# PSUM banks of the expert stage sorted by role, with banks of their own for h of each expert's first tile

## The chip, the cores and the metric

The kernel runs on one core of a Trainium2 chip. The core has five instruction queues that run side by side and meet through semaphores: TensorE (PE, matrix products and transposes), VectorE (DVE), ScalarE (ACT), GpSimd (POOL) and SyncE (SP, which starts most DMA transfers). PE writes its results to PSUM, which has eight banks of 2 KB on each of 128 partitions. The metric is device time in microseconds (us) of one execution. Stated is the median of several runs.

## What is computed

Attention over 16 heads with a block-causal mask, a dense feed-forward layer, and then a mixture of eight experts with one expert per token. The change is in the last part:

```python
def _moe2_ref(x, w_gate, w1, w2, capacity):       # x: 1152 x 512, 8 experts, capacity 288
    logits = x @ w_gate
    expert_idx = np.argmax(logits, axis=1)
    probs = softmax(logits)                        # written out in the original
    gate_w = probs[np.arange(N), expert_idx]
    # token i takes the next free slot of its expert, if one is left: disp[e, slot] = x[i]
    h = np.maximum(np.einsum('ecd,edf->ecf', disp, w1), 0.0)    # w1: 8 x 512 x 1024
    y = np.einsum('ecf,efd->ecd', h, w2)                        # w2: 8 x 1024 x 512
    out[i] = gate_w[i] * y[expert_idx[i], pos[i]]               # 0 for tokens without a slot
```

## The kernel before

The kernel has three parts: attention (`part1`), the feed-forward layer with the router (`part2`), and the experts (`part3`). Parts one and two take the first 340 us. In `part3` every engine executes its instructions in the order in which the code is written; a tile framework adds the semaphore waits that the data and the reuse of buffers need. A pool with `bufs=2` hands out two buffers in turn, and the first instruction that writes a buffer waits until the readers of its last content are done.

Each float32 product is made of three passes: a number is split into a high and a low part (`xh`, `xl` for weights, `dh`, `dl` for tokens, `gh`, `gl` for the hidden layer), and high*high, high*low and low*high are added. ACT makes the high parts, DVE the low ones (line 87 is the helper for that).

The loop of `part3` runs over the experts e. The slots of an expert lie in three tiles j of 128, 128 and 32 slots; `compute(e, j)` is called an *arm* here. Arm 0 runs if the expert has any token, arm 1 if it has more than 128 and arm 2 if it has more than 256. The conditions are branches that each engine takes for itself from a count loaded into its registers (line 1251). An arm that is not taken has a stand-in on each engine that waits until that engine's work so far is done and then adds to the engine's semaphore counter what the arm would have counted. In the profile, waits for it and for the branch appear as `ACTq L1288`, `PEq L1288` and the like: the queue of that engine, not an instruction of it.

An arm does on PE, in this order: 12 matmuls for the first half of the hidden layer (`hx`, line 1193), 6 for the second half, four transposes `hT` of the first half (line 1204), 6 more `hx`, 6 matmuls of the second layer (`acc`, line 1214), `hT` of the second half, 6 `acc`, in arm 0 the transposes `dT` of the next expert's tile 0 (line 1163), and 12 `acc`. Between them ACT applies the relu (`hr`, line 1199, from the `hx` bank), makes `gh` from `hT` (line 1208) and scales the result (`o`, line 1240, from `acc`); DVE makes `gl` from `hT` and `gh`. `o` then goes to the output by an indirect DMA from POOL. In arm 0 six of eight pieces of the next expert's weights are converted as well: `side` gives ACT's halves (`xh`, line 1116) and DVE's (`xl`) to `run` at fixed places of the arm, three of each at its beginning, ahead of the first `hr` on ACT and the first `gl` on DVE. The last two pieces are converted behind arm 0.

Between arm 0 of one expert and arm 0 of the next stand, on every engine: arm 1 or its stand-in, `turn_slots(e + 1, 1)` (four `dT`, then `dh` on ACT and `dl` on DVE), arm 2 or its stand-in, `turn_slots(e + 1, 2)`, and the load of the next count.

The PSUM pools of `part3` have two banks each: `ps_acc` for `acc`, `ps_l1` for `hx`, `ps_m` for `hT` and for `dT` of tile 0, `ps_t` for `dT` of tiles 1 and 2.

Of the kernel before, what the change touches and what calls it, by code (L numbers as in the profile page):

```python
# [9 lines left out]
FP32 = mybir.dt.float32  # L10
# [7 lines left out]
PSUM = bass.MemoryType.PSUM  # L18
# [24 lines left out]
def attention_ffn_moe(  # L43
# [19 lines left out]
    KD = DM // 128  # L63
# [22 lines left out]
    def split_lo(eng, lo, x, hi):  # L86
        eng.tensor_tensor(out=lo, in0=x, in1=hi.bitcast(FP32), op=ALU.subtract)  # L87
# [1032 lines left out]
    def part3():  # L1120
        y_stack.close()
        p3 = ExitStack()
# [1 line left out]
        raw_q = p3.enter_context(tc.tile_pool(name="raw_q", bufs=8, side="right"))  # L1124
        dp = p3.enter_context(tc.tile_pool(name="dp", bufs=2, side="right"))
        hp = p3.enter_context(tc.tile_pool(name="hp", bufs=2, side="right"))
        ps_acc = p3.enter_context(tc.tile_pool(name="ps_acc3", bufs=2, space=PSUM))
        ps_l1 = p3.enter_context(tc.tile_pool(name="ps_l13", bufs=2, space=PSUM))
        ps_m = p3.enter_context(tc.tile_pool(name="ps_m3", bufs=2, space=PSUM))
        ps_t = p3.enter_context(tc.tile_pool(name="ps_t3", bufs=2, space=PSUM))  # L1130
        stiles = [(128 * i, min(128, CP - 128 * i)) for i in range(CT)]
        dT = state["dT"]
# [25 lines left out]
        def turn_slots(e, j):  # L1158

            r, (hi, lo), gt, (s0, n) = rows[e], dT[j], gate[e], stiles[j]  # L1160
            ps = (ps_t if j else ps_m).tile([128, KD, 128], FP32, tag="m", name="dT")
            for kk in range(KD):
                nc.tensor.transpose(  # L1163
                    out=ps[:, kk, 0:n], in_=r[0:n, j, kk * 128:(kk + 1) * 128], identity=ident[0:n, 0:n]
                )
            nc.scalar.activation(out=hi, in_=ps[:, :, 0:n], func=ACTF.Copy)
            split_lo(nc.vector, lo, ps[:, :, 0:n], hi)
            nc.gpsimd.tensor_copy(out=gt[0:n, j, 0:1], in_=r[0:n, j, DM:DM + 1])  # L1168
            nc.gpsimd.tensor_copy(out=gt[0:n, j, 1:2].bitcast(I32), in_=r[0:n, j, DM + 1:DM + 2].bitcast(I32))  # L1169

        def passes(x, w):
            return [(x[0], w[0]), (x[0], w[1]), (x[1], w[0])]

        def compute(e, j, side=(), turn_next=lambda: None):


            s0, n = stiles[j]
            h, hr, g = {}, {}, {}
            his, los = ([x[y] for x in side] for y in range(2))
            acc = ps_acc.tile([128, DM], FP32, tag="acc", name="acc")  # L1180

            def run(fs, k):
                for f in fs[:k]:
                    f()
                del fs[:k]

            def l1(c, half):

                if half == 0:
                    h[c] = ps_l1.tile([128, 512], FP32, tag="l1", name="hx")  # L1190
                todo = [(x, y, kk) for x, y in ((0, 0), (0, 1), (1, 0)) for kk in range(KD)]
                for i, (x, y, kk) in list(enumerate(todo))[6 * half:6 * half + 6]:
                    nc.tensor.matmul(  # L1193
                        out=h[c][0:n], lhsT=dT[j][x][:, kk], rhs=xw[e, 2 * kk][y][:, 0, c * 512:(c + 1) * 512],
                        start=(i == 0), stop=(i == len(todo) - 1),
                    )
                if half == 1:
                    hr[c] = hp.tile([128, 512], FP32, tag="hr", name="hr", bufs=3)
                    nc.scalar.activation(out=hr[c][0:n], in_=h[c][0:n], func=ACTF.Relu)

            def turn(c):
                ps = ps_m.tile([128, 4, 128], FP32, tag="m", name="hT")
                for i in range(4):
                    nc.tensor.transpose(  # L1204
                        out=ps[:, i, 0:n], in_=hr[c][0:n, i * 128:(i + 1) * 128], identity=ident[0:n, 0:n]
                    )
                g[c] = gh, gl = [hp.tile([128, 4, 128], F32R, tag="g" + x, name="g" + x) for x in "hl"]
                nc.scalar.activation(out=gh[:, :, 0:n], in_=ps[:, :, 0:n], func=ACTF.Copy)  # L1208
                split_lo(nc.vector, gl[:, :, 0:n], ps[:, :, 0:n], gh[:, :, 0:n])

            def l2(c, half):
                for f in range(4 * c + 2 * half, 4 * c + 2 * half + 2):
                    for i, (x, y) in enumerate(passes(g[c], xw[e, f // 2 * 2 + 1])):
                        nc.tensor.matmul(  # L1214
                            out=acc[0:n], lhsT=x[:, f % 4, 0:n], rhs=y[:, f % 2, :],
                            start=(f == 0 and i == 0), stop=(f == NF - 1 and i == 2),
                        )

            run(his, 3)
            run(los, 3)  # L1220
            l1(0, 0)
            l1(0, 1)
            run(his, 1)
            l1(1, 0)
            turn(0)
            run(his, 1)
            run(los, 2)
            l1(1, 1)
            l2(0, 0)
            run(his, 1)  # L1230
            turn(1)
            run(los, 1)
            l2(0, 1)
            run(his, NX)
            turn_next()
            run(los, NX)
            l2(1, 0)
            l2(1, 1)
            y = hp.tile([128, DM], FP32, tag="hr", name="o", bufs=3)
            nc.scalar.mul(y[0:n], acc[0:n], gate[e][0:n, j, 0:1])  # L1240
            nc.gpsimd.indirect_dma_start(  # L1241
                out=views[e * CT + j],
                out_offset=bass.IndirectOffsetOnAxis(ap=gate[e][0:n, j, 1:2].bitcast(I32), axis=0),
                in_=y[0:n],
                in_offset=None,
                bounds_check=NT - 1,
                oob_is_err=False,
            )
# [10 lines left out]
        for e in range(E):  # L1259
# [10 lines left out]
            def turn_next():  # L1270
                if new:
                    turn_slots(e + 1, 0)
# [14 lines left out]
            for j in range(1, CT):  # L1287
                with tc.If(count[e] > 128 * j):  # L1288
                    compute(e, j)
                if new:  # L1290
                    turn_slots(e + 1, j)
# [12 lines left out]
    with tc.manual_schedule(engines=every):  # L1304
        part3()
# [27 lines left out]
```

## Time and profile before

| | before |
|---|---|
| median of 3 runs | 520.35 us (519.45 to 522.28) |
| the profiled execution | 521.78 us |
| its span, first to last instruction | 520.1 us |
| PE busy | 493.7 us (95%) |
| DVE busy | 341.7 us (66%) |
| ACT busy | 312.0 us (60%) |
| POOL busy | 117.2 us (23%) |

The profiler recorded one execution. The difference between its time and its span lies before the first and behind the last instruction. A timeline row gives the start, the time, the engine, the line, the operation, the tile written, the tiles read and the number of instructions merged into the row; what stands in brackets is the time that the engine sat idle just before, and what ended it. PE's matmuls overlap, so the time of a single one is longer than the distance from one to the next. The granted clock is the share of full speed that the chip gave TensorE in a stretch; it has two levels, 1.2 and 2.4 GHz, and shares between one half and one are mixtures.

Twelve arms run with this input: arm 0 of experts 0 to 6, arm 1 of experts 0, 4, 5 and 6, and arm 2 of expert 5. Expert 7 has no token.

### The profile page before, as it was taken

To read this page: it belongs to the slowest core of one execution; us is meant where nothing else is said; L and a number is where in the kernel's file an instruction comes from. 1 tells how busy PE (TensorE), PEld (TensorE's weight loads), DVE (VectorE), ACT (ScalarE), POOL (GpSimd) and SP (SyncE) were. 2 spreads that over 40 slices of the span, in tenths; PEclk is the share of its full clock that TensorE was granted. 3 is DMA by queue.
4 is the path that set the end of the run, shared out by engine and by line. 5 is a ranking of instruction groups with operands and counts; after the bars stand their busy time and mean duration, and the time that the engine had idled before them with its cause. 6 is when DMAs were issued, how large, how long until landed. Compare 5 with 4: busy or idle time off the path is not lost. (4 is left out here: it accounts for less than half of the span.)

```text
span 520.1 us, 8710 instructions
## 1 busy us (share of the span) xinstructions
PE 493.7 (95%) x2842; PEld 409.2 (79%) x2842; DVE 341.7 (66%) x828; ACT 312.0 (60%) x699; POOL 117.2 (23%) x219
## 2 busy tenths in 40 slices
PE   7999999999999999999999999889989989999994
PEld 6678877879998889888898888767767768786683
DVE  4479898969987999974554366563565866461351
ACT  4569898867866656753553455374656765562551
POOL 6266777651000000000000112500131230100211
PEclk9589999999999999999999999889979889999999
DMA  8757766503789884430140043377488767180110
GB/s 195 171 125 189 188 146 151 151 4 122 186 256 227 266 284 139 121 122 0 42 122 2 14 129 142 103 255 301 152 299 314 273 245 276 55 337 20 30 43 23
DMA packets 61254, 80.86 MB, mean 155 GB/s; under 512 B 33170, under 2 KB 33170, under 8 KB 61200
## 3 DMA queue, kind: packets, MB, share of 16 engines
q1 hardware_dynamic: 58368, 75.18, 47.9%
q0 software_dynamic: 1632, 4.72, 2.4%
q8 instruction: 28, 0.46, 0.4%
q10 hardware_dynamic: 1200, 0.30, 0.3%
q14 instruction: 26, 0.21, 0.1%
HBM read 62.17 MB, written 12.41 MB: 143 GB/s over the span
## 5 line engine op out<-in xcount | busy, mean ns | idle before, releaser
L260 PE MATMUL acc<-wbh,gh 128*128 128x512 f32 x144 | 57.3, 398 | 0.0
L260 PE MATMUL acc<-wbh,gl 128*128 128x512 f32 x144 | 57.1, 397 | 0.0
L260 PE MATMUL acc<-wbl,gh 128*128 128x512 f32 x144 | 57.1, 397 | 0.0
L904 POOL DMA_INDIRECT disp<-y_all,slot x9 | 9.1, 1013 | 201.1 <-DVE e L245 178.3
L87 DVE TENSOR_TENSOR xl<-rb,xh 128x1024 fp32r<-128x1024 f32 (+1 forms) x36 | 38.9, 1100 | 22.2 <-ACT xh L1116 22.2
L476 POOL TENSOR_SCALAR prob<-prob,stat 128x576 f32<-128x576 f32 (+3 forms) x80 | 41.9, 536 | 35.7 <-DVE stat L470 21.5
L449 ACT ACTIVATE prob<-s,stat 128x288 f32<-128x288 f32 (+4 forms) x96 | 45.3, 479 | 1.7 <-DVE stat L464 1.1
L243 ACT ACTIVATE e<-h 128x384 f32<-128x384 f32 x48 | 23.2, 483 | 36.4 <-PE h L233 34.0
L186 DVE SCALAR_TENSOR_TENSOR cv_t<-r,cv_t 128x512 int32<-128x512 int32 x64 | 44.1, 689 | 0.3
L87 DVE TENSOR_TENSOR xl<-ra,xh 128x1024 fp32r<-128x1024 f32 (+1 forms) x36 | 39.3, 1101 | 7.1 <-ACT xh L1116 6.2
L233 PE MATMUL h<-xh,wah 128*128 128x384 f32 x192 | 42.3, 341 | 0.9 <-DVE e L245 0.9
L436 DVE TENSOR_REDUCE stat<-s 128x1 f32<-128x288 f32 (+4 forms) x96 | 37.7, 422 | 8.2 <-PE s L425 5.7
L233 PE MATMUL h<-xl,wah 128*128 128x384 f32 x192 | 41.6, 337 | 0.0
L233 PE MATMUL h<-xh,wal 128*128 128x384 f32 x192 | 41.1, 336 | 0.0
L245 DVE SCALAR_TENSOR_TENSOR e<-e,h 128x384 f32<-128x384 f32 x48 | 26.3, 549 | 21.2 <-ACT e L244 21.0
L1214 PE MATMUL acc<-xh,gh 128*128 128x512 f32 (+1 forms) x96 | 39.3, 410 | 0.0
L1193 PE MATMUL hx<-xh,dh 128*128 128x512 f32 (+1 forms) x96 | 30.3, 442 | 9.4 <-ACTq L1288 7.2
L233 PEld LDWEIGHTS h<-xh,wah 128*128 128x128 f32 x192 | 34.1, 188 | 6.2 <-DVE e L245 2.4
L1241 POOL DMA_INDIRECT out<-o,gt x12 | 11.7, 972 | 117.7 <-ACT o L1240 40.5
L1214 PE MATMUL acc<-xh,gl 128*128 128x512 f32 (+1 forms) x96 | 38.0, 395 | 0.0
L1214 PE MATMUL acc<-xl,gh 128*128 128x512 f32 (+1 forms) x96 | 37.8, 394 | 0.0
L87 DVE TENSOR_TENSOR gl<-hT,gh 128x512 fp32r<-128x512 f32 (+1 forms) x24 | 15.8, 658 | 33.4 <-ACT gh L1208 33.4
(171 smaller groups left out, 1204.5 us busy)
## 6 DMA issues: line engine op xcount, KB each, us to landing
ra<-in_moe_w SPq DMA_DIRECT2D x32, 512.0 KB, 5.5
rb<-in_moe_w SPq DMA_DIRECT2D x32, 512.0 KB, 6.4
r<-in_moe_w_in SPq DMA_DIRECT2D x16, 512.0 KB, 5.4
r<-in_moe_w_out SPq DMA_DIRECT2D x16, 512.0 KB, 4.0
disp<-z SPq DMA_DIRECT2D x18, 257.0 KB, 6.8
rows<-disp SPq DMA_DIRECT2D x14, 257.0 KB, 3.2
out<-z SPq DMA_DIRECT2D x9, 256.0 KB, 4.3
kr<-in_k SPq DMA_DIRECT2D x16, 128.0 KB, 2.6
```

The source lines that it names most:

```text
L87: eng.tensor_tensor(out=lo, in0=x, in1=hi.bitcast(FP32), op=ALU.subtract)
L186: nc.vector.scalar_tensor_tensor(out=st["t"], in0=x(), scalar=scalar, in1=st["t"], op0=op, op1=ALU.bitwise_or)
L233: nc.tensor.matmul(out=h[:, f, :], lhsT=w[:, kk, (f0 + f) * 128:(f0 + f + 1) * 128], rhs=x[:, kk, t0:t0 + n], start=(i == 0), stop=(i == l ...
L243: nc.scalar.activation(out=e, in_=hf, func=ACTF.Relu, scale=-1.0)
L245: nc.vector.scalar_tensor_tensor(out=e, in0=e, scalar=-1.0, in1=hf, op0=ALU.add, op1=ALU.max)
L260: nc.tensor.matmul(out=acc[t], lhsT=x[:, f, t * 128:(t + 1) * 128], rhs=w[:, f0 + f, :], start=(first and f == 0 and i == 0), stop=(last a ...
L436: nc.vector.tensor_reduce(out=stat[n][0][0:nq, t + b:t + b + 1], in_=banks[n, part, b][0:nq, c0:c0 + w], axis=AX.X, op=ALU.max, negate=True,)
L449: nc.scalar.activation(out=prob[n, part][0:nq, c0 + k0:c0 + k0 + w], in_=banks[n, part, b][0:nq, c0:c0 + w], func=ACTF.Exp, bias=stat[n][0 ...
L476: nc.gpsimd.tensor_scalar(out=p, in0=p, scalar1=stat[n][2][0:nq, t:t + 1], scalar2=0.0, op0=ALU.mult, op1=ALU.add)
L1193: nc.tensor.matmul(out=h[c][0:n], lhsT=dT[j][x][:, kk], rhs=xw[e, 2 * kk][y][:, 0, c * 512:(c + 1) * 512], start=(i == 0), stop=(i == len( ...
L1214: nc.tensor.matmul(out=acc[0:n], lhsT=x[:, f % 4, 0:n], rhs=y[:, f % 2, :], start=(f == 0 and i == 0), stop=(f == NF - 1 and i == 2),)
L1241: nc.gpsimd.indirect_dma_start(out=views[e * CT + j], out_offset=bass.IndirectOffsetOnAxis(ap=gate[e][0:n, j, 1:2].bitcast(I32), axis=0), ...
```

## The change

PSUM has eight banks before and after. `ps_acc` and `ps_m` go from two banks to one each. `ps_l1` becomes a list of two pools of two banks: the first for `hx` of arm 0, the second for `hx` of arms 1 and 2. `dT` of tile 0 moves from `ps_m` to `ps_t`, which then serves `dT` of all three tiles with two banks.

```diff
-        ps_acc = p3.enter_context(tc.tile_pool(name="ps_acc3", bufs=2, space=PSUM))
-        ps_l1 = p3.enter_context(tc.tile_pool(name="ps_l13", bufs=2, space=PSUM))
-        ps_m = p3.enter_context(tc.tile_pool(name="ps_m3", bufs=2, space=PSUM))
+        ps_acc = p3.enter_context(tc.tile_pool(name="ps_acc3", bufs=1, space=PSUM))
+        ps_l1 = [p3.enter_context(tc.tile_pool(name=f"ps_l1{i}3", bufs=2, space=PSUM)) for i in range(2)]
+        ps_m = p3.enter_context(tc.tile_pool(name="ps_m3", bufs=1, space=PSUM))
         ps_t = p3.enter_context(tc.tile_pool(name="ps_t3", bufs=2, space=PSUM))
...
-            ps = (ps_t if j else ps_m).tile([128, KD, 128], FP32, tag="m", name="dT")
+            ps = ps_t.tile([128, KD, 128], FP32, tag="m", name="dT")
...
-                    h[c] = ps_l1.tile([128, 512], FP32, tag="l1", name="hx")
+                    h[c] = ps_l1[j > 0].tile([128, 512], FP32, tag="l1", name="hx")
```

No instruction is added, removed or moved on any engine; what changes is which semaphores instructions wait for, and up to what count. On PE, at the passage from expert 0 to expert 1, there stands before the change (`dh_2031` and `dl_2032` are the two halves of tile 0's tokens; names ending in `_49` are the engines' and DMA queues' semaphores):

```order
L1163 MATMUL dT<-ident,rows 128x32 [waits DMAHW6_49]
L1163 MATMUL dT<-ident,rows 128x32 x3
L1251 TENSOR_LOAD count
L1251 ISA x2
L1274 COMPARE_AND_BRANCH
L1193 MATMUL hx<-xh,dh_2031 128x512 [waits Activation_49]
L1193 MATMUL hx<-xh,dh_2031 128x512 x3
L1193 MATMUL hx<-xl,dh_2031 128x512 [waits DVE_49] x4
L1193 MATMUL hx<-xh,dl_2032 128x512 [waits DVE_49]
```

And at the same place after the change, where the lines are two higher:

```order
L1165 MATMUL dT<-ident,rows 128x32 [waits DMAHW6_49,DVE_49,PE_49]
L1165 MATMUL dT<-ident,rows 128x32 x3
L1253 TENSOR_LOAD count
L1253 ISA x2
L1276 COMPARE_AND_BRANCH
L1195 MATMUL hx<-xh,dh_2031 128x512 [waits Activation_49]
L1195 MATMUL hx<-xh,dh_2031 128x512 x3
L1195 MATMUL hx<-xl,dh_2031 128x512 x4
L1195 MATMUL hx<-xh,dl_2032 128x512 x4
```

The last `dT` waits for DVE as well, and the waits of `hx` for DVE, which that one covers, are gone. The first `hx` waits for ACT's semaphore both times, but up to another count: 477 before, which is reached inside arm 2 (or by its stand-in), and 468 after, which is reached with `o` of arm 0.

## Rows read from the trace of the kernel before

**Rows 1.** Who waited for whom from 340 to 520 us, PE: us in all, times, longest

```profile
PE hx L1193 <- ACTq L1288: 7.2, 5, 2.0
```

**Rows 2.** PE's timeline from expert 2 to expert 3 (B)

```profile
401.84 0.41 PE L1163 MATMUL dT<-ident,rows 32*128 32x32 f32 x4 [0.30 <-DMA rb<-in_moe_w]
404.30 1.59 PE L1193 MATMUL hx<-xh,dh 128*128 128x512 f32 x4 [2.05 <-ACTq L1288]
...
410.15 0.60 PE L1204 MATMUL hT<-ident,hr 128*128 128x128 f32 x4
...
412.45 0.39 PE L1214 MATMUL acc<-xh,gl 128*128 128x512 f32 x1
```

**Rows 3.** PE's timeline at other experts

```profile
362.70 0.66 PE L1204 MATMUL hT<-ident,hr 128*128 128x128 f32 x4 [0.96 <-ACT hr L1199]
...
385.31 2.08 PE L1193 MATMUL hx<-xh,dh 128*128 128x512 f32 x4 [2.05 <-ACTq L1288]
...
392.30 0.60 PE L1204 MATMUL hT<-ident,hr 128*128 128x128 f32 x4
...
427.90 0.60 PE L1204 MATMUL hT<-ident,hr 128*128 128x128 f32 x4
...
442.21 0.40 PE L1214 MATMUL acc<-xh,gh 128*128 128x512 f32 x1
...
449.13 0.40 PE L1163 MATMUL dT<-ident,rows 32*128 32x32 f32 x4 [0.30 <-PEq L1288]
450.00 1.19 PE L1193 MATMUL hx<-xh,dh 128*128 128x512 f32 x4 [0.47 <-ACTq L1288]
...
454.28 0.60 PE L1204 MATMUL hT<-ident,hr 128*128 128x128 f32 x4
```

**Rows 4.** Stretches: us, busy us by engine (count), granted clock, DMA share, GB/s

```profile
385.00:392.00 7.00, 6.68 (x17) 5.32 (x18) 5.37 (x6) 4.55 (x7) 3.23 (x5) 0.55 0.72 189
404.00:411.00 7.00, 6.70 (x24) 5.37 (x25) 5.36 (x6) 5.14 (x8) 2.65 (x5) 0.76 0.72 213
...
357.00:364.00 7.00, 6.04 (x31) 4.71 (x30) 2.07 (x3) 2.39 (x4) 0.00 (x0) 1.00 0.59 226
```

**Rows 5.** ACT's timeline

```profile
362.05 0.60 ACT L1199 ACTIVATE hr<-hx 128x512 f32<-128x512 f32 x1 [2.42 <-DMA out<-o,gt]
...
381.87 0.69 ACT L1240 ACTIVATE o<-acc,gt 128x512 f32<-128x512 f32 x1 [2.24 <-PEq L1288]
...
400.85 0.69 ACT L1240 ACTIVATE o<-acc,gt 128x512 f32<-128x512 f32 x1 [2.25 <-PEq L1288]
401.44 1.99 ACT L1116 ACTIVATE xh<-rb 128x1024 fp32r<-128x1024 f32 x2
403.60 0.60 ACT L1166 ACTIVATE dh<-dT 128x512 fp32r<-128x512 f32 x1 [0.17 <-ACTq L1288]
...
406.73 1.04 ACT L1116 ACTIVATE xh<-ra 128x1024 fp32r<-128x1024 f32 x1
...
418.69 0.69 ACT L1240 ACTIVATE o<-acc,gt 128x512 f32<-128x512 f32 x1 [2.24 <-PEq L1288]
...
436.44 0.69 ACT L1240 ACTIVATE o<-acc,gt 128x512 f32<-128x512 f32 x1 [2.24 <-PE acc L1214]
```

**Rows 6.** DVE's timeline

```profile
389.73 1.22 DVE L87 TENSOR_TENSOR xl<-ra,xh 128x1024 fp32r<-128x1024 f32 x1
...
398.63 0.69 DVE L87 TENSOR_TENSOR dl<-dT,dh 128x512 fp32r<-128x512 f32 x1
402.51 2.36 DVE L87 TENSOR_TENSOR xl<-rb,xh 128x1024 fp32r<-128x1024 f32 x2 [3.19 <-ACT xh L1116]
...
409.08 1.22 DVE L87 TENSOR_TENSOR xl<-ra,xh 128x1024 fp32r<-128x1024 f32 x1
411.46 0.69 DVE L87 TENSOR_TENSOR gl<-hT,gh 128x512 fp32r<-128x512 f32 x1 [1.16 <-ACT gh L1208]
...
426.55 1.22 DVE L87 TENSOR_TENSOR xl<-ra,xh 128x1024 fp32r<-128x1024 f32 x1
```

## The prediction

> **What bounds the kernel now.** I read the page first: TensorE (PE) is busy nearly all the time, so only two things can be gained, PE's idle time and time in which its clock is low. The change touches only the expert stage (340 us to the end). So I took, for that stage, the view of who waited for whom, on PE alone: its largest entry is the first h matmul of an expert waiting for ACT's instruction queue, 7.2 us in five waits [rows 1]. The reader is to see that the releaser is "ACTq", not an ACT instruction: PE waits until ACT has *gone past* something. PE's timeline at such a place [rows 2] shows a wait of 2.05 us between the last dT and the first hx, and after it four hx matmuls that take 1.59 us where four take 1.19 us at another expert [rows 3]. The table of stretches says why: the granted clock is 0.55 and 0.76 of full speed in the 7 us behind two such waits, and 1.00 in a stretch with a wait of 0.96 us [rows 4]. So a boundary between two experts costs the wait and then a stretch in which part of the matmuls run at the lower level, 1.2 GHz instead of 2.4.
>
> Why PE waits: h of arm 0 of the next expert takes the bank that h of arm 2 had. Arm 2 (slots from 256 on) is mostly not taken, but its stand-in on ACT, which makes up the missing counts, must be reached: ACT runs o, two late xh, dh of tile 1, then the stand-in [rows 5]. dh starts at 403.60, ends at 404.20, and hx starts at 404.30. In the compiled program the first hx waits for ACT's counter at 477 before (a count inside arm 2) and at 468 after (o of arm 0).
>
> Seven boundaries lie between eight experts. At three (after experts 1, 2 and 3) neither further arm is taken, and the wait is 2.05 us; I call them A, B and C. At two (into experts 1 and 5) arm 1 was taken and the wait is about 0.5 us, at one all arms are taken and there is none, and the last expert has no rows at all.
>
> **The change part by part.** *h of arm 0 in banks of its own.* After it the first hx needs ACT only up to o, which starts at 400.85 in B and is over before dT of tile 2 is. What is left on PE is its own sequence: load the count, branch. Its price is at most 0.87 us, from the start of that dT to hx, 449.13 to 450.00 [rows 3]. In B, hx can then start at 401.84 + 0.87 = 402.71 instead of 404.30: 1.59 us earlier. At the two boundaries with waits of about 0.5 us nothing is won: there this same sequence is already what takes the time. A bound on the other side is 0 us, if ACT is what releases hx there too; then these two give up to 0.5 us each, a value I don't take.
>
> *What is late next.* The gain at hx is not the gain at the end. From hx to the first hT PE needs 4.28 us at full clock (450.00 to 454.28 [rows 3]), so it would be there at 402.71 + 4.28 = 406.99. But hT needs hr, and hr stands on ACT behind three conversions of the next expert's weights (xh), which do not move, since ACT's chain from o on waits for PE nowhere. The third starts at 406.73. Queued xh follow each other by 0.95 us (two take 1.99, one alone 1.04 [rows 5]), so hr starts at 407.68, that is o + 6.83. From hr to hT it takes 0.65 us (362.05 to 362.70, where PE waited for just that [rows 3, 5]). So hT comes at o + 7.48, and PE gets a **new wait** of 408.33 - 406.99 = 1.3 us. The same offsets hold in A and C, where o starts at 381.87 and 418.69 [rows 5]:
> - A: hT at 389.35 instead of 392.30: 2.95 us.
> - B: hT at 408.33 instead of 410.15: 1.82 us.
> - C: hT at 426.17 instead of 427.90: 1.73 us [rows 2, 3].
>
> Next comes the third matmul of acc, which needs gl on DVE, and this stands behind three xl. It follows hT by 2.30 us (410.15 to 412.45 [rows 2]), so it is due at o + 9.78. The third xl starts at 389.73, 409.08, 426.55; with 1.14 us from start to start (two take 2.36, one 1.22) and 0.69 for gl [rows 6], gl ends at o + 9.69 in A and C, in time, and at o + 10.06 in B. There about 0.33 us are given back. From there on PE has work up to the arm's end: the second hr and gl stand behind fewer conversions, and in the trace of before PE does not wait there.
>
> Sum: 2.95 + (1.82 - 0.33) + 1.73 = **6.2 us**. It holds both gains, the wait and the clock, cut to what ACT and DVE allow. Without that cut it would be the waits and the slow stretches in full: 3 x 1.6, and for the clock, from hx to hT, 6.99 - 4.28 = 2.71 in A (385.31 to 392.30), 5.85 - 4.28 = 1.57 in B (404.30 to 410.15) [rows 2, 3] and about as much in C, 10.6 us; this is no end of the range, since ACT's order is fixed.
>
> *acc in one bank.* The first acc matmul of an arm must wait for o of the arm before it. o starts at 436.44, acc of the next arm at 442.21 [rows 3, 5]: 5 us of hx lie between. Nothing, and it would cost only if ACT were 5 us late.
>
> *hT in one bank.* hT of half 1 must wait for gl of half 0. The acc matmuls ahead of it on PE wait for the same gl already. Nothing.
>
> *dT of all three tiles in two banks.* dT of tile 2 now waits for dl of tile 0: that starts at 398.63 [rows 6] and lasts 0.69, dT of tile 2 starts at 401.84. Cover 2.5 us; nothing. The dT of tiles 0 and 1 wait for reads of the expert before. Behind these waiting transposes stand all later matmuls, so a lost cover would go to the end in full.
>
> The DMAs are not moved by an instruction. They get 2 us less per expert at three experts, and the weights are loaded more than an arm ahead.
>
> Profiled execution: 521.78 us, of which 520.1 is the span; 521.78 - 6.2 = 515.6. The median of the runs is 520.35 (519.45 to 522.28), so the same saving gives **514.2**.
>
> **The rivals.**
> *The clock still falls at the boundary.* Idle time of about 0.30 + 0.5 us remains around short dT. For: it falls behind 2.05 us of waiting. Against: behind 0.30 + 0.47, with the same dT, the next four hx run at full pace, 1.19 us [rows 3]. Then the slow stretch stays but begins 1.59 us earlier, PE reaches hT no earlier than ACT, and each boundary gives about 1.55: 4.6 in all, 515.7.
>
> *The clock falls behind the new wait.* 1.3 us at hT is longer than the longest wait without a fall (0.96 us, clock 1.00 [rows 3, 4]) and shorter than 2.05. Nothing in the trace lies between. A fall at the price of B, 1.57, at three places takes 4.7 of the 6.2: 518.9.
> The Trainium skill, "TensorE: Matmul & The Clock Gate", section "A second HAM failure mode: psum-queue depth-cycling", says that brief idling of PE between groups of matmuls, as a kernel cycles through PSUM banks, can make the clock fall and rise over and over. It speaks against a change that spreads PE's idle time over two shorter gaps. By that rule the sum would be this rival's. The 0.96 us row does not bear it out; no row decides it for 1.3 us.
>
> *Slower.* The same mechanism at the price of A, where the clock stayed low longer: 2.71 at each hT of three experts, 8.1 us against 6.2 won: 522.3. It decides from 2.06 us per place. Against it: behind the new wait PE has a full arm of dense matmuls, as in B.
>
> *The change does not do what it says.* The first hx still waits for a count of ACT; if another tile of this matmul took the wait over, the time stays at 520.35. Against: the count it waits for is now one that ACT passes before PE is there.
>
> **How the numbers follow.** My forecast 0.57; clock falls at the boundary 0.13; clock falls at hT 0.20; slower 0.05; no effect 0.05. The low end is 514.2 less the scatter of the runs (520.35 - 519.45 = 0.9) and 0.5 for terms that I took at nothing: 512.8. The high end takes in two or nearly three falls behind the new wait: 518.6; outside it lie about a third of that rival and the last two. About 0.5% (2.6 us, so 517.75) is what a measurement of this kernel can tell from no change. Faster by over that: the forecast, the first rival and half of the second, less some scatter, 0.77; within it 0.17; slower 0.06.
>
> **What would show it.** Right: the entry "hx waits for ACTq" is gone from PE's waits; a new one, hT waits for hr, of about 1.3 us at three places; the granted clock near 1.00 over the first 7 us of experts 2, 3 and 4; hT at o + 7.5; no wait of acc for o, none of dT for dl. Wrong: a granted clock well under 1 behind the three hT waits (the second rival), or three waits of hx that remain.

## The result

The changed kernel takes 513.48 us (511.65 to 518.14) against 519.31 us (516.60 to 522.69) of the kernel before on the same chip, 20 runs of each. The ratio is 0.9895, 95% interval [0.9877, 0.9914]: of 520.35 us that is 5.5 us (4.5 to 6.4). 514.2 was forecast, with 6.2 us saved.

The profiled execution of after took 514.5 us, 512.8 of it the span. The first lines of its page (busy time, share of the span, instructions) answer to the small table of before:

```profile
span 512.8 us, 8712 instructions
PE 487.3 (95%) x2842; PEld 403.3 (79%) x2842; DVE 341.3 (67%) x828; ACT 311.7 (61%) x699; POOL 118.0 (23%) x219
```

Over the whole kernel PE's busy time fell by 6.4 us (493.7 to 487.3) with the same number of products, and its idle time by 0.9 us (520.1 - 493.7 = 26.4 before, 512.8 - 487.3 = 25.5 after). Part of this lies ahead of the change. For the stretch across A, B and C alone, from `o` of arm 0 of expert 1 to that of expert 4, the two rows are, before and after (us; busy us of PE, PEld, DVE, ACT, POOL with counts; granted clock, DMA share, GB/s):

```profile
381.87:436.44 54.57, 47.16 (x206) 37.25 (x207) 36.94 (x39) 36.41 (x48) 14.05 (x21) 0.87 0.81 285
379.77:429.17 49.40, 43.58 (x206) 33.79 (x207) 36.77 (x39) 36.02 (x49) 14.01 (x21) 0.97 0.86 310
```

Of the 5.17 us won there, 3.58 are matmuls that take less time, and 1.59 are less waiting.

Who waited for whom from 335 to 513 us, PE (us in all, times, longest), which answers to [rows 1]:

```profile
PE hT L1206 <- ACT hr L1201: 3.3, 3, 1.2
PE dT L1165 <- PEq L1290: 2.8, 9, 0.4
PE hx L1195 <- DVE dl L87: 2.3, 1, 2.3
PE hx L1195 <- issue: 1.1, 2, 0.7
PE hx L1195 <- ACTq L1290: 0.9, 2, 0.4
PE hx L1195 <- ACT xh L1116: 0.9, 2, 0.4
```

The five waits of hx for ACT's queue, 7.2 us, are down to two of 0.4 us, those at the boundaries into experts 1 and 5. The new entry is hT waiting for hr: two of its three times are at A and B, and the third, 1.2 us, is in arm 1 of expert 0, where this wait was 0.96 us before. "issue" is a wait for nothing that the profile shows; one of the two is 0.65 us and has a part below.

PE's timeline at the boundaries A (into expert 2) and C (into expert 4). B is like A. These rows answer to [rows 2, 3]:

```profile
379.99 0.63 PE L1165 MATMUL dT<-ident,rows 128*128 128x128 f32 x4 [0.30 <-PEq L1290]
380.91 0.40 PE L1165 MATMUL dT<-ident,rows 32*128 32x32 f32 x4 [0.30 <-PEq L1290]
381.74 1.19 PE L1195 MATMUL hx<-xh,dh 128*128 128x512 f32 x4 [0.43 <-issue]
...
385.57 0.63 PE L1195 MATMUL hx<-xl,dh 128*128 128x512 f32 x2
387.24 0.66 PE L1206 MATMUL hT<-ident,hr 128*128 128x128 f32 x4 [1.04 <-ACT hr L1201]
...
389.60 0.41 PE L1216 MATMUL acc<-xh,gl 128*128 128x512 f32 x1
...
413.98 0.95 PE L1195 MATMUL hx<-xh,dh 128*128 128x512 f32 x3 [0.43 <-ACT xh L1116]
415.58 0.40 PE L1195 MATMUL hx<-xh,dh 128*128 128x512 f32 x1 [0.65 <-issue]
415.82 1.64 PE L1195 MATMUL hx<-xl,dh 128*128 128x512 f32 x4
417.26 1.91 PE L1195 MATMUL hx<-xh,dl 128*128 128x512 f32 x4
...
420.62 0.60 PE L1206 MATMUL hT<-ident,hr 128*128 128x128 f32 x4
```

In A the first four hx come 0.83 us behind dT of tile 2 and take 1.19 us, four at full speed. PE then stands 1.04 us ahead of hT. In C a standstill of 0.65 us follows the third hx, and the next eight take 1.64 + 1.91 us; hT has no wait there.

The stretches of 7 us behind hx at A, B and C, and behind hT at A, B and C (us; busy us of PE, PEld, DVE, ACT, POOL with counts; granted clock, DMA share, GB/s), which answer to [rows 4]:

```profile
381.40:388.40 7.00, 5.62 (x25) 4.37 (x26) 6.39 (x7) 6.49 (x10) 4.07 (x7) 1.00 0.61 187
397.50:404.50 7.00, 5.62 (x25) 4.37 (x26) 6.40 (x7) 6.49 (x9) 3.94 (x7) 1.00 0.67 214
413.70:420.70 7.00, 6.07 (x19) 4.65 (x20) 6.41 (x7) 6.09 (x8) 4.04 (x7) 0.76 0.64 193
387.20:394.20 7.00, 6.96 (x36) 5.73 (x37) 6.89 (x8) 5.02 (x7) 1.70 (x2) 1.00 0.99 362
403.30:410.30 7.00, 6.98 (x37) 5.72 (x38) 6.90 (x8) 5.00 (x7) 1.68 (x2) 1.00 0.99 368
420.60:427.60 7.00, 7.00 (x38) 5.82 (x37) 5.86 (x7) 4.39 (x7) 0.47 (x1) 1.00 1.01 370
```

The clock is at 1.00 except behind hx in C, where it is a mixture of both levels.

ACT's and DVE's rows at A, which answer to [rows 5, 6]:

```profile
379.77 0.69 ACT L1242 ACTIVATE o<-acc,gt 128x512 f32<-128x512 f32 x1 [2.24 <-PEq L1290]
...
385.66 1.05 ACT L1116 ACTIVATE xh<-ra 128x1024 fp32r<-128x1024 f32 x1
386.61 0.58 ACT L1201 ACTIVATE hr<-hx 128x512 f32<-128x512 f32 x1
...
388.77 0.68 DVE L87 TENSOR_TENSOR gl<-hT,gh 128x512 fp32r<-128x512 f32 x1
```

hr starts at o + 6.84, straight behind the third conversion.

To see where the time went I take `o` of arm 0 from one expert to the next, on ACT: the distances across A, B and C are 18.98, 17.84 and 17.75 us before, 54.57 in sum, and 16.08, 16.08 and 17.24 after, 49.40 in sum. That is 5.17 us less: 2.90, 1.76 and 0.51. The spans differ by 7.3 us. The rest lies ahead of A: 1.64 us before the first hx, in parts of the program that the change does not touch, and 0.5 in expert 0. From `o` of expert 4 to the end both kernels take the same time. The sum over A, B and C leaves out the parts ahead of it, which scatter by 5 us from one execution to the next (the first `o` comes between 349.5 and 354.5 us in the profiles of this document). I give it for every kernel beside the ratio. But it is one execution of each kernel, and that of before took 521.78 us, 2.5 us above the median of its 20 runs, so what a sum shows against 54.57 may be too much; the ratio decides.

### The profile page after: what moved, and what is told of

Same layout as the page of the kernel before. It is cut to its first block, busy times and chain, and to the rows that moved or that the text cites. A ratio compares the mean times of both kernels' runs of the same rounds, so it can differ in the third digit from the quotient of the medians.

```text
span 512.8 us, 8712 instructions
## 1 busy us (share of the span) xinstructions
PE 487.3 (95%) x2842; PEld 403.3 (79%) x2842; DVE 341.3 (67%) x828; ACT 311.7 (61%) x699; POOL 118.0 (23%) x219
## 5 line engine op out<-in xcount | busy, mean ns | idle before, releaser
L245 DVE SCALAR_TENSOR_TENSOR e<-e,h 128x384 f32<-128x384 f32 x48 | 26.4, 550 | 21.2 <-ACT e L244 21.0
L1116 ACT ACTIVATE xh<-ra 128x1024 fp32r<-128x1024 f32 (+1 forms) x36 | 34.3, 961 | 5.0 <-PE h L233 2.8
L249 ACT ACTIVATE gh<-e 128x384 fp32r<-128x384 f32 x48 | 25.1, 522 | 16.7 <-DVE e L245 16.1
```

Source lines behind the costliest of these rows:

```text
L245: nc.vector.scalar_tensor_tensor(out=e, in0=e, scalar=-1.0, in1=hf, op0=ALU.add, op1=ALU.max)
L249: nc.scalar.activation(out=gh, in_=ef, func=ACTF.Copy)
L1116: lambda: nc.scalar.activation(out=hi, in_=r, func=ACTF.Copy),
```

## The experiments

**Fewer banks, or the banks of h?** The change does two things: it shrinks `acc` and `hT` to one bank and moves dT, and it gives h of arm 0 its own banks. The first experiment does the first alone, the second hands the freed banks to all arms in turn, four in a ring. The diff is that of the first; the second has `bufs=4` in the same place.

```diff
-        ps_l1 = [p3.enter_context(tc.tile_pool(name=f"ps_l1{i}3", bufs=2, space=PSUM)) for i in range(2)]
+        ps_l1 = p3.enter_context(tc.tile_pool(name="ps_l13", bufs=2, space=PSUM))
...
-                    h[c] = ps_l1[j > 0].tile([128, 512], FP32, tag="l1", name="hx")
+                    h[c] = ps_l1.tile([128, 512], FP32, tag="l1", name="hx")
```

> Only the small pools: acc one bank, hT one bank, dT of all tiles in two banks, but h of all arms still takes turns in one pool of two banks; two of the eight banks are not used at all. Theory (the small pools cost nothing, the gain is all in h's own banks): as the kernel before, ratio 1.000 within 0.3%, and PE's first hx still waits some 7 us for ACT's queue. Rival (the small pools cost something, and h's own banks give more than the whole change): ratio above 1.004. Rival (they give part of the gain): below 0.996.

> The small pools, and h in one pool of four banks that all arms use in turn: the number of banks without the roles. Arm 0 of the next expert then takes the banks that arm 1 had, not arm 2, so PE waits until ACT has passed arm 1's stand-in, o + 2.7 us, where the changed kernel starts hx at o + 1.8. Theory (what decides is when ACT reaches hr, o + 7.5): hx at o + 2.7 plus 4.28 is still earlier than hr, so the time is that of the changed kernel, ratio 0.988 to 0.991, if the clock does not fall behind the longer wait; if it does, each of the three places gives 0.7 us instead of 2, ratio 0.995. Rival (only banks of the role's own help): ratio 1.000.

The small pools alone: ratio 1.0009 [0.9985, 1.0033], sum 54.37 us. PE's waits from 335 to 520 us, the two largest entries:

```profile
PE hx L1195 <- ACTq L1290: 6.5, 5, 1.9
PE hx L1195 <- DVE dl L87: 2.3, 1, 2.3
```

The old wait is back, and no new one has come with one bank for `acc`, one for `hT` and two for all dT. The four in a ring: ratio 0.9943 [0.9918, 0.9968], sum 50.23 us. Its first hx waits 1.13 us at each boundary. PE's rows at A and B, and the stretches behind A, B and C:

```profile
381.22 1.20 PE L1195 MATMUL hx<-xh,dh 128*128 128x512 f32 x4 [1.13 <-ACTq L1290]
397.32 2.07 PE L1195 MATMUL hx<-xh,dh 128*128 128x512 f32 x4 [1.14 <-ACTq L1290]
```

```profile
381.20:388.20 7.00, 6.66 (x30) 5.11 (x30) 6.42 (x9) 6.57 (x9) 3.68 (x6) 1.00 0.68 222
397.30:404.30 7.00, 6.98 (x25) 5.63 (x26) 5.85 (x7) 5.83 (x8) 2.99 (x6) 0.76 0.74 214
414.30:421.30 7.00, 6.93 (x25) 5.60 (x26) 5.90 (x7) 5.78 (x8) 3.63 (x6) 0.76 0.65 194
```

The same four banks in another arrangement give about half of the gain. The ring's bank belonged to arm 1 last, so hx waits for that arm's stand-in on ACT, which stands behind the two late conversions. So the number of banks shortens the wait, and the roles remove it. Behind equal waits the clock fell in two cases of three, and there over half of the gain was lost: from `o` to `o` it is 16.10 us across A, as good as the changed kernel's 16.08, and 17.06 and 17.07 across B and C. In A hx starts 0.7 us later than in the changed kernel, and hT still comes at o + 7.47, because it waits for hr:

```profile
386.01 0.66 PE L1206 MATMUL hT<-ident,hr 128*128 128x128 f32 x4 [0.33 <-ACT hr L1201]
```

**The wait or the clock?** Both gains end at the same hT. To part them, the next kernel keeps the old wait (small pools, no banks of its own for h) and lets PE work through it: 24 short products into a bank of their own, of which nothing is used, ahead of h of arm 0 at A, B and C.

```diff
+            if j == 0 and e in (2, 3, 4):
+                for _ in range(24):
+                    nc.tensor.matmul(out=warm[:, 0:128], lhsT=mrow, rhs=mrow, start=True, stop=True)
```

> As shrink, and one of the free banks takes 24 dummy matmuls of 128 columns on PE ahead of h of arm 0 of experts 2, 3 and 4, in the time in which PE waits for ACT's queue anyway. The wait stays in full; only the fall of the clock behind it should go. Theory (most of the gain is the clock): hx starts as late as before and hT comes 4.28 us after it, 2.7, 1.6 and 1.5 us earlier than before: ratio 0.989, nearly that of the change. Rival (the wait itself is what is worth something): ratio 1.000, with the granted clock at 1.00 all the same.

Measured: ratio 0.9942 [0.9911, 0.9972], sum 49.71 us, and the granted clock is 1.00 behind all three boundaries. At A a standstill of PE came among the idle products:

```profile
382.03 0.45 PE L1187 MATMUL warm<-mrow 128*128 128x128 bf16 x5 [0.43 <-ACT xh L1116]
383.08 1.22 PE L1187 MATMUL warm<-mrow 128*128 128x128 bf16 x19 [0.60 <-issue]
384.11 1.18 PE L1200 MATMUL hx<-xh,dh 128*128 128x512 f32 x4
```

To see whether this belongs to the work or to the place in the program, the same kernel ran with 66 instead of 42 products at the program's very start, which puts 24 more products, each with its weight load, ahead of all later instructions of PE:

```diff
-        for _ in range(42):
+        for _ in range(66):
```

> This is the kernel with the PSUM pools of after cut to two banks and 24 dummy products of bf16 ahead of h of arm 0 of experts 2, 3 and 4 (they compute nothing of the result), and with 66 instead of 42 products at the program's start, so that every later instruction of PE stands 24 places further on. Theory (the gain is the clock that did not fall; the 0.60 us in which PE stood behind the branches of the boundary into expert 2 belong to the place in the program): the standstill at A is gone or at another place, the stretches from o to o of arm 0 are about 16.3 us each, 49 us in sum against 49.4 of after and 54.4 of the kernel with the small pools alone, and the ratio to before is about 0.991. Rival (the standstill belongs to the work ahead of it): it stands at A again with 0.6 us, the first stretch is 17.0 us, and the ratio is 0.994 as without the shift.

Ratio 0.9927 [0.9896, 0.9959], sum 16.30 + 16.46 + 16.30 = 49.06 us; the standstill is gone:

```profile
376.09 0.69 ACT L1247 ACTIVATE o<-acc,gt 128x512 f32<-128x512 f32 x1 [2.24 <-PEq L1295]
...
378.07 1.51 PE L1187 MATMUL warm<-mrow 128*128 128x128 bf16 x24 [0.45 <-ACT xh L1116]
379.54 1.20 PE L1200 MATMUL hx<-xh,dh 128*128 128x512 f32 x4
...
383.83 0.60 PE L1211 MATMUL hT<-ident,hr 128*128 128x128 f32 x4
```

Here hx starts as late as before, at o + 3.45, and yet hT comes at o + 7.74, where before it came at o + 10.43 in A. The changed kernel, with hx 1.5 us earlier, is there at o + 7.47. In this trace the clock thus carries most of the gain: 54.57 - 49.06 = 5.5 us, of 6.3 that the change gives where no standstill disturbs it (below). The earlier start adds 0.8, because ACT's order cuts off the rest. The timed runs give the clock less. This execution took 510.47 us and was the fastest of its 11 runs, whose median is 515.48; the ratios of the two kernels with idle products are worth 3.0 and 3.8 us, against 5.5 for the change. So the clock carries somewhat over half by the ratios, with wide intervals, and the rest is not accounted for row by row. The converse, an earlier start with the clock down, was not run by itself. At B and C of the ring hx came 0.77 us earlier than before, the clock fell, and the stretches were 0.78 and 0.68 us shorter, so the shares depend on the order in which the two gains are counted.

**What cuts off the gain, and the clock behind the new wait.** If hr behind three conversions of the next expert's weights sets hT, fewer of them ahead of it must move hT forward, and more must lengthen the wait. The second also tests the main rival, that the clock falls behind a wait at hT. The number in these two lines changes from 3 to 2, 4 and 1:

```diff
-            run(his, 3)
-            run(los, 3)
+            run(his, 2)
+            run(los, 2)
```

> The changed kernel with two instead of three conversions ahead of the first hr on ACT and the first gl on DVE; the third comes later in the arm. Theory (behind the change, ACT's conversions ahead of hr and DVE's ahead of gl set the time): hr comes 0.95 us earlier, hT at o + 6.5, and the third acc 0.95 us earlier at each of three boundaries, 2.8 us in all beyond the change: ratio 0.983 to 0.985. Rival (the new wait at hT costs nothing, something else holds the arm): ratio as the change, 0.989.

> The changed kernel with four conversions ahead of the first hr and gl instead of three: PE's wait at hT grows from 1.05 to 2.0 us. Theory of the prediction (ACT's order sets hT): hT 0.95 us later at three boundaries, ratio 0.989 + 0.0055 = 0.995, if the clock stands a single gap of 2 us in an arm. Rival two of the prediction (the clock falls behind the wait at hT): it does so here if anywhere, granted clock well under 1 in the 7 us behind hT of experts 2, 3 and 4, and up to 1.6 us more at each: ratio 1.000 to 1.004.

> The changed kernel with one conversion ahead of the first hr and gl. Theory: hr no longer waits for ACT's conversions, hT follows hx by PE's own 4.28 us, at o + 6.1 against o + 6.5 with two and o + 7.5 with three; 0.4 us per boundary beyond two, ratio 0.982. Rival (the conversions put back to the end of the arm now hold dh, dl and so the dT of the next tiles): no better than with two, ratio 0.985 or above, and PE waits of dT for DVE or ACT.

Two: ratio 0.9848 [0.9814, 0.9883], sum 15.13 + 15.27 + 17.01 = 47.41 us. A and B are another 0.9 us shorter each. In C the 0.68 us standstill and the fall of the clock take it back. It beats both kernels.

Four: ratio 1.0016 [0.9994, 1.0038], sum 51.65 us. PE's row at A, and the stretches behind hT at A, B and C:

```profile
389.59 0.66 PE L1206 MATMUL hT<-ident,hr 128*128 128x128 f32 x4 [1.91 <-ACT hr L1201]
```

```profile
389.60:396.60 7.00, 7.00 (x36) 5.62 (x37) 5.79 (x7) 4.00 (x6) 0.70 (x1) 1.00 0.99 376
406.80:413.80 7.00, 7.00 (x36) 5.58 (x37) 5.78 (x7) 4.00 (x6) 0.70 (x1) 1.00 1.02 403
424.00:431.00 7.00, 7.00 (x36) 5.58 (x37) 5.75 (x7) 4.01 (x6) 0.73 (x1) 1.00 1.02 380
```

Waits of 1.87 to 2.00 us inside an arm, and the clock stays at 1.00 behind all three. That refutes the main rival beyond the 1.05 us of the changed kernel. The forecast of 0.995 failed all the same. The ratio is near 1 although the three boundaries are 2.9 us shorter than in the trace of before: arm 0 of the other experts waits for its first hr as well, and from the last arm of experts 0, 4 and 5 to the next `o` this kernel takes some 2 us more than after. The rest is not accounted for; in the two profiled executions this kernel is 2.1 us ahead of before (519.65 against 521.78), in the medians 1.1 us behind it (519.55 against 518.47).

One: ratio 0.9871 [0.9832, 0.9911], sum 49.85 us. There is no wait at hT, but a new one of dT for DVE, which now has the low halves to make ahead of it. PE's rows at A and the stretch behind:

```profile
377.83 0.63 PE L1165 MATMUL dT<-ident,rows 128*128 128x128 f32 x4 [0.30 <-DVE xl L87]
379.02 0.40 PE L1165 MATMUL dT<-ident,rows 32*128 32x32 f32 x4 [0.56 <-DVE xl L87]
379.87 1.97 PE L1195 MATMUL hx<-xh,dh 128*128 128x512 f32 x4 [0.45 <-issue]
```

```profile
379.80:386.80 7.00, 6.93 (x25) 5.58 (x26) 4.05 (x5) 4.29 (x7) 2.42 (x7) 0.76 0.61 191
```

The clock fell at all three boundaries (0.76 each) behind about 0.30 + 0.56 + 0.45 us of idle time around the short dT, less than the 2 us in one piece that it outlasted in the kernel with four.

**The standstill at C.** The 0.65 us behind the third hx of expert 4 were in no sum. The changed kernel ran with the 24 more products at the program's start ("shifted by 24" below), the kernel with two conversions likewise, and both ran once more as they were.

> The changed kernel with 24 more warm-up matmuls at the very start (66 instead of 42), so that everything behind stands 48 PE instructions later in the program. In the changed kernel's trace PE stands still for 0.65 us inside the first hx of expert 4, behind its third matmul and with nothing that the profile shows it to wait for, and the clock falls there; that boundary gave 0.5 us instead of 1.7. Theory (the standstill belongs to a place in the program, as an instruction fetch would): it is gone from there or moved 48 instructions earlier; where it then falls under a running stretch or a wait, the clock at expert 4 stays at 1.00 and the segment from o to o is 16.1 us as at experts 2 and 3: 1.2 us less than the change, ratio 0.987. Rival (it belongs to this arm, whatever the place, say to a transfer): the same standstill behind the third hx, ratio 0.9895.

> Two conversions ahead of hr and 24 more warm-up matmuls, both in the changed kernel. Theory: the two gains add, 2.8 us and 1.2 us beyond the change, ratio 0.982. Rival (the standstill stays at expert 4): as with two conversions alone, ratio 0.985.

> This is the changed kernel itself once more, for its ratio and for one question: does PE stand for 0.65 us behind the third product of h at the boundary into expert 4 in every execution, or was that one execution? Theory (it belongs to the place in the program): about 0.65 us at the same product, the granted clock of the 7 us from there about 0.76, the three stretches from o to o 16.1, 16.1 and 17.2 us. Rival (chance of one execution): no standstill there, or at another boundary, and 16.1 us three times. Either way the ratio to before is 0.988 to 0.991.

> The changed kernel with two conversions of the following pair ahead of hr in place of three, once more. Theory: ratio to before 0.983 to 0.988, 2 us less than the changed kernel on the same chip (two boundaries at 1.0 us less each, the third about 0.2), with a standstill of about 0.7 us behind the third product of h of expert 4 again. Rival (the gain of two conversions was a chance of one chip): equal to the changed kernel within 0.3%.

| | ratio to before | A, B, C and sum, us | standstill at C, us | clock behind hx at C |
|---|---|---|---|---|
| after | 0.9895 [0.9877, 0.9914] | 16.08, 16.08, 17.24: 49.40 | 0.65 | 0.76 |
| after, again | 0.9889 [0.9859, 0.9920] | 16.08, 16.08, 16.10: 48.26 | about 0.24 | 1.00 |
| after, shifted by 24 | 0.9881 [0.9833, 0.9930] | 16.11, 16.07, 16.09: 48.27 | none | 1.00 |
| two conversions | 0.9848 [0.9814, 0.9883] | 15.13, 15.27, 17.01: 47.41 | 0.68 | 0.76 |
| two, again | 0.9827 [0.9795, 0.9859] | 15.10, 15.37, 15.30: 45.77 | 0.34 | 1.00 |
| two, shifted by 24 | 0.9857 [0.9814, 0.9899] | 15.10, 15.11, 15.14: 45.35 | none | 1.00 |

PE's rows at C in the second execution of after, where four hx take 1.43 us instead of 1.19 (hence the 0.24), and in that of two conversions:

```profile
414.01 1.43 PE L1195 MATMUL hx<-xh,dh 128*128 128x512 f32 x4 [0.43 <-issue]
...
419.51 0.66 PE L1206 MATMUL hT<-ident,hr 128*128 128x128 f32 x4 [0.81 <-ACT hr L1201]
```

```profile
409.95 0.95 PE L1195 MATMUL hx<-xh,dh 128*128 128x512 f32 x3 [0.43 <-ACT xh L1116]
411.24 0.40 PE L1195 MATMUL hx<-xh,dh 128*128 128x512 f32 x1 [0.34 <-issue]
```

Neither theory held as written. The place in the program bears on it: four executions of two kernels show a standstill at C, the same two kernels shifted show none there, and the shift also removed the one at A among the idle products. But the place is not all. The kernels with four conversions and with one have PE's instructions in the same order, without a shift, and show next to none at C: the four hx take 1.24 and 1.20 us. And its length differs between executions of one kernel (0.65 and 0.24 us, 0.68 and 0.34); only the longer ones brought the clock down. In the second execution of after the three boundaries give 54.57 - 48.26 = 6.31 us. In the ratios the shift cannot be told from no shift. The kernel with two conversions is the fastest that was run: 2.4 and 3.2 us ahead of the changed kernel by the ratios of the two pairs without a shift, and 1.2 us, within the intervals, with it.

## Why the prediction was right

*What waits.* The forecast was that hx no longer waits for arm 2's stand-in, and starts 0.87 us behind dT of tile 2: it was 0.83. It took "no effect" out. From `o` hx came at 1.97 instead of the 1.86 of the forecast, since dT of tile 2 itself comes at o + 1.14 now and not at o + 0.99. The kernel with the small pools alone has the 1.14 as well, so this small cost is theirs; ACT's order hid it.

*The new bound.* hT was forecast at o + 7.48, set by three conversions ahead of hr on ACT. It came at o + 7.47 in A (387.24 - 379.77) and in B, and in the kernels with two and four conversions it moved by about a conversion each way. hr was forecast at o + 6.83 and was at 6.84. The new wait was forecast at 1.3 us and is 1.04 and 1.06 in A and B. The forecast counted from start to start: hx at 381.74 plus 4.28 is 386.02, 1.22 ahead of hT. The profile counts idle time from the end of the last hx, 386.20.

*The term of B.* 0.33 us were to be given back, as gl was forecast to end at o + 10.06. It starts 9.01 behind o, as in A, and nothing was given back: 1.76 us instead of 1.49. The delay on DVE in the trace of before was taken for a property of this expert. It is a wait of 0.50 us ahead of a dl, which DVE has neither in A and C of that trace nor in B of after; what it waited for there is not shown:

```profile
405.38 0.69 DVE L87 TENSOR_TENSOR dl<-dT,dh 128x512 fp32r<-128x512 f32 x1 [0.50 <-DVEq L1288]
```

*The term of C* is the one that was mis-sized: 0.51 us instead of 1.73 in the profiled execution, through the standstill of 0.65 us and the slow matmuls behind it. It is the first rival (the clock still falls at the boundary) at one place of three, by a cause that the rival did not name. In the second execution C gave 1.65, and the sum of 6.31 stands against 6.2. That the timed gain, 5.5 us, lies a little below fits such falls in some of the executions, and also the slow profiled execution of before; since only one profile of each series exists, how often they come was not measured.

*The clock.* The sum took both gains together and cut them at ACT's bound, which made it right without saying which of them carries it. The idle products give the clock 5.5 of 6.3 us in the traces, and 3.0 to 3.8 of 5.5 in the ratios: the larger part, by an amount that stays open. The prediction speaks of an hx that starts 1.59 us earlier as the first step; with the clock kept up, that start added 0.8 us in the traces and some 2 in the ratios.

*The main rival*, a fall behind the new wait, had 0.20. The clock was 1.00 behind 1.04 us at hT, and behind 1.87 to 2.00 us in the kernel with four conversions. The Trainium skill, "TensorE: Matmul & The Clock Gate", section "A second HAM failure mode: psum-queue depth-cycling", tells of a kernel in which brief idling of PE between groups of matmuls makes the clock fall and rise. These rows at hT do not bear that out; the falls behind 1.13 us in the ring and behind the short gaps with one conversion are nearer to it.

*Terms at nothing.* The smaller pools cost nothing that can be measured (1.0009 with an interval of 0.24% either way), so the covers that were named for them held, but for the 0.15 us at dT of tile 2.

## What to carry to other kernels

A wait of PE is to be priced with the granted clock of the stretch behind it: here 2 us of waiting were followed by 1.5 to 2.7 us more than full speed takes from hx to hT, and keeping PE busy through the wait won, by the ratios, over half of what removing it won. When a wait is removed, follow the next instruction that is needed back to its engine's own order: the place of hr behind three conversions gave the time of hT to within 0.01 us in A and B, and moving it past one of them won 0.7 to 1.0 us at each of the two, about the 0.95 us that one conversion takes on ACT. In a ring of PSUM banks the wait is for the last reader of the bank that is next, so banks sorted by who releases them late removed a wait that as many banks in a common ring only shortened.

## What the chip showed that was not expected

Behind which idle time the clock fell at A, B and C, from all profiles without idle products:

| idle time of PE at the boundary, us | clock of the 7 us behind |
|---|---|
| 0.30 + 2.05 ahead of hx (before), 0.30 + 0.30 + 1.83 to 1.91 (small pools) | 0.55 to 0.78, 6 of 6 |
| 0.30 + 0.30 + 1.13 (four in a ring) | 1.00, 0.76, 0.76 |
| 0.30 + 0.30 + 0.43, standstill of 0.65 or 0.68 after three hx | 0.76, 2 of 2 |
| the same with a standstill of 0.24 or 0.34 | 1.00, 2 of 2 |
| about 0.30 + 0.56 + 0.45 (one conversion) | 0.76, 3 of 3 |
| 0.30 + 0.30 + 0.42 to 0.51, no standstill | 1.00, 17 of 17 |
| 1.87 to 2.00 in one piece at hT, inside an arm (four conversions) | 1.00, 3 of 3 |

No length of idle time sorts these cases: 1.3 us around the short transposes brought the clock down three times, and 2 us between long matmuls did not in three cases. Equal waits (the ring) went both ways. What decides it is not settled here.

The standstill of PE for 0.2 to 0.7 us behind skipped branches, with nothing in the profile that it waits for, went away when 24 more products stood far ahead of it, and also, without them, in the kernels with four conversions and with one. What PE waits for there, and why the length varies, stays open.
